# SiLU written with tanh instead of sigmoid, and plain transposes in one part of the attention, in a fused attention and SwiGLU kernel

## The chip, the cores and the metric

The kernel runs on one NeuronCore of a Trainium2 chip. The metric is device time in microseconds (us), the median of several executions. A run also leaves a profile of one execution. Its engines are PE (TensorE matmul), PEld (TensorE weight load), DVE (VectorE), ACT (ScalarE), POOL (GpSimd) and SP (SyncE, which issues transfers here).

## The reference

```python
# q, k, v: 8 batches, 8 heads, 576 rows, 64 columns, float32; tau = 0.02
scores = q @ k.T / 8
thresh = max(scores, axis=-1) - tau
scores = where(scores >= thresh, scores, -1e9)
attn   = exp(scores - max(scores))
attn   = attn / (sum(attn) + 1e-9)
x      = (attn @ v), heads side by side        # 4608 x 512
g      = x @ w_gate                            # 512 x 1536
out    = (g * sigmoid(g) * (x @ w_val)) @ w_out
```

## The kernel before

Attention is worked off in tiles of 128 query rows (the last tile of a batch's head pair has 64 rows of both heads). For each tile TensorE makes scores, VectorE takes the maximum, ScalarE the exponential, VectorE the threshold with its row sum. The feed-forward work of earlier rows is cut into pieces, and a pacing rule puts some of them between the tiles (`fill`), so that TensorE has work while the softmax chain of a tile runs. Score banks (`ps_s`) hold one full tile, so the next tile's scores wait until the threshold instruction has read the last one (19 waits of TensorE, 33.3 us). Four more PSUM banks (`ps_f`) serve everything else.

The first batch has no feed-forward work at first and is computed with whole rows; its probabilities are turned by TensorE. Each turn is a matmul against a diagonal that holds the reciprocals of the row sums, so it normalises at the same time. The turn of a tile's probabilities is called its flip here:

```python
diags = dbufs[0][:, 0:m, :]                       # in scores(), first batch
for x in range(m):
    nc.scalar.activation(diags[:, x, :], ident, AF.Copy, scale=ri[:, x:x + 1])
...
end = ps_f.tile([P, 512], F32, ...)               # in flip()
for h, (p, diag) in enumerate(ps):
    tp = ps_f.tile([P, 512], F32, ...)
    for kt in range(KT):                          # four blocks of 128 x 128
        nc.tensor.matmul(tp[:, kt * P:(kt + 1) * P], p[:, kt * P:(kt + 1) * P], diag, start=True, stop=True)
    nc.tensor.matmul(end[...], p[:, KM:S], diag, ...)
    nc.scalar.copy(pT[:, h], tp...)
```

Later batches ("halved" tiles) use VectorE's transposes (`L371`, 754 ns for 128x576), and GpSimd and ScalarE normalise (`L352`, `L354`) before them.

The gate part copies the gate out of PSUM; the value part multiplies the value by the raw gate; the sigmoid comes later, in groups, because a change between it and the exponential costs a table load; the trace has 38 at `L520` and 37 at `L525`, 1283 ns each:

```python
nc.scalar.copy(gts[...], ps)                                          # gate()
nc.vector.tensor_tensor(out=hts[f // 2], in0=gts[...], in1=ps, op=ALU.mult)   # value()
...
def sigmoids():
    ...                                                    # returns when nothing waits
    eng = nc.vector if attended else nc.gpsimd
    for hts, gt, own in unsig:
        nc.scalar.activation(gt, gt, AF.Sigmoid)           # L520, with a table load before
        for y, (x, ht) in enumerate(own):
            eng.tensor_tensor(out=ht, in0=ht, in1=gt..., op=ALU.mult)         # L522
    if not attended:
        nc.scalar.activation(idle, tau_s, AF.Exp)          # L525, loads the exponential's tables back
    ...                                                    # differences for a seven-product scheme, GpSimd
# main loop, per tile:
    next(go); fill(part); next(go)
    if len(unsig) >= SIG:        # SIG = 3
        sigmoids()
    fill(part); next(go)         # this step emits L352 and L354
```

## Time and profile before

| | before |
|---|---|
| median of 3 runs | 1570.57 us (1569.39 to 1570.74) |
| TensorE busy | 1509.2 of 1568.6 us (96%) |
| ScalarE, VectorE, GpSimd busy | 832, 1022, 628 us |

The groups by line, of which these are the ones that the change touches (columns: line, engine, operation, output and input, count, then busy us and mean ns of one, then idle us of the engine before them and who ended it):

```profile
L504 DVE TENSOR_TENSOR ht<-gt,pv 128x512 f32<-128x512 f32 x102 | 69.8, 685 | 125.0 <-PE pv L481 116.2 <-ACT sums L275 5.9 <-ACT gt L497 2.4
L497 ACT COPY gt<-pg 128x512 f32<-128x512 f32 x108 | 63.5, 588 | 79.7 <-PE pg L481 77.3 <-POOL pall L352 1.8
L520 ACT ACT_TABLE_LOAD x38 | 48.8, 1283 | 8.2 <-DVE ht L504 6.5 <-DVE tot L343 1.1
L525 ACT ACT_TABLE_LOAD x37 | 47.5, 1283 | 0.7
L389 PE MATMUL tp<-pall 128*128 128x128 f32 x288 | 43.5, 296 | 1.3 <-ACT xall L418 0.8 <-ACT pall L361 0.4 <-ACT gt L497 0.2
```

The 75 table loads take 96 us of ScalarE, and the turning matmuls (tp) take 43.5 us of TensorE, the full engine. Whether ScalarE's 96 us matter is a question of waits. The waits of TensorE (who waited for whom, us, times, longest):

```profile
PE sc L296 <- DVE pall L336: 33.3, 19, 3.4
PE sc L301 <- DVE qT L768: 8.0, 1, 8.0
...
PE po L595 <- POOL ht L522: 4.8, 1, 4.8
```

The 8.0 us are the start. Nearly all the rest of TensorE's waiting is for the threshold instruction to free the score banks (3.8 us more of it stand under L301), and once for a gate multiply on GpSimd. No table load is named.

### The profile page before, as it was taken

To read this page: it belongs to the slowest core of one execution; us is meant where nothing else is said; L and a number is where in the kernel's file an instruction comes from. 1 tells how busy PE (TensorE), PEld (TensorE's weight loads), DVE (VectorE), ACT (ScalarE), POOL (GpSimd) and SP (SyncE) were. 2 spreads that over 40 slices of the span, in tenths; PEclk is the share of its full clock that TensorE was granted. 3 is DMA by queue.
4 is the path that set the end of the run, shared out by engine and by line. 5 is a ranking of instruction groups with operands and counts; after the bars stand their busy time and mean duration, and the time that the engine had idled before them with its cause. 6 is when DMAs were issued, how large, how long until landed. Compare 5 with 4: busy or idle time off the path is not lost. (4 is left out here: it accounts for less than half of the span.)

```text
span 1568.6 us, 31607 instructions
## 1 busy us (share of the span) xinstructions
PE 1509.2 (96%) x11872; PEld 1141.3 (73%) x11872; DVE 1022.2 (65%) x3150; ACT 832.2 (53%) x2165; POOL 628.3 (40%) x638
## 2 busy tenths in 40 slices
PE   7999878999999999999999999999999999899998
PEld 5777554467677767777777777777777777788887
DVE  6866877777677757774767777777676777412212
ACT  5767766546465555654555555474647464511110
POOL 2313543336546354633454544363536263500011
PEclk9999999999999999999999999999999999999999
DMA  8533311211111111110211111111011120000000
GB/s 189 142 99 102 95 28 31 56 43 30 24 45 45 31 32 45 43 34 1 45 32 45 31 45 31 45 32 36 12 42 31 45 46 15 1 14 0 14 14 14
DMA packets 176489, 66.93 MB, mean 43 GB/s; under 512 B 159696, under 2 KB 159696, under 8 KB 176336
## 3 DMA queue, kind: packets, MB, share of 16 engines
q1 hardware_dynamic: 168656, 54.88, 15.7%
q0 software_dynamic: 2944, 9.44, 1.7%
q8 instruction: 94, 1.54, 0.4%
q10 hardware_dynamic: 4736, 0.59, 0.3%
q14 instruction: 59, 0.48, 0.1%
HBM read 55.44 MB, written 9.44 MB: 41 GB/s over the span
## 5 line engine op out<-in xcount | busy, mean ns | idle before, releaser
L481 PE MATMUL pv<-xall,wgv 128*128 128x256 f32 x1728 | 405.7, 386 | 0.0
L481 PE MATMUL pg<-xall,wgv 128*128 128x256 f32 x1728 | 399.9, 382 | 0.0
L481 PEld LDWEIGHTS pv<-xall,wgv 128*128 128x128 f32 x1728 | 328.4, 192 | 67.0 <-issue 21.7
L481 PEld LDWEIGHTS pg<-xall,wgv 128*128 128x128 f32 x1728 | 323.5, 190 | 66.4 <-issue 19.0
L352 POOL TENSOR_SCALAR pall<-pall,ri 128x288 f32<-128x288 f32 x252 | 249.9, 1002 | 258.3 <-DVE ri L346 234.0
L336 DVE SCALAR_TENSOR_TENSOR pall<-sc,th,pall 128x288 f32<-128x288 f32 (+1 forms) x540 | 258.6, 529 | 63.6 <-ACT pall L332 63.6
L332 ACT ACTIVATE pall<-sc,nm 128x288 f32<-128x288 f32 (+1 forms) x540 | 236.1, 509 | 0.5
L296 PE MATMUL sc<-kT,qT 64*32 64x288 f32 x4032 | 161.6, 416 | 34.8 <-DVE pall L336 33.3
L316 DVE TENSOR_REDUCE mx<-sc 128x2 f32<-128x576 f32 x252 | 177.7, 742 | 22.3 <-PE sc L296 21.1
L371 DVE STREAM_TRANSPOSE pall<-pall 128x576 f32<-128x576 f32 x252 | 181.9, 754 | 10.7 <-POOL pall L352 10.7
L522 POOL TENSOR_TENSOR ht<-ht,gt 128x512 f32<-128x512 f32 x84 | 104.7, 1272 | 200.9 <-ACT gt L520 200.9
L275 ACT COPY sums<-sums 32x4 f32<-32x4 f32 (+1 forms) x560 | 108.5, 194 | 143.7 <-DVE pall L336 134.2
L595 PE MATMUL po<-wo,ht 128*128 128x256 f32 x768 | 176.8, 382 | 0.0
L595 PEld LDWEIGHTS po<-wo,ht 128*128 128x128 f32 x768 | 144.9, 191 | 28.0 <-issue 4.6
L354 ACT ACTIVATE pall<-pall,ri 128x288 f32<-128x288 f32 x252 | 122.2, 527 | 69.6 <-DVE ri L346 68.5
L504 DVE TENSOR_TENSOR ht<-gt,pv 128x512 f32<-128x512 f32 x102 | 69.8, 685 | 125.0 <-PE pv L481 116.2
L328 ACT ACTIVATE th<-nm,cut 128x4 f32<-128x4 f32 (+1 forms) x140 | 41.2, 295 | 206.1 <-DVE nm L319 206.0
L296 PEld LDWEIGHTS sc<-kT,qT 64*32 64x32 f32 x4032 | 58.6, 106 | 114.7 <-issue 83.5
L438 PE MATMUL xa<-pall,vall 64*64 64x288 f32 x2016 | 130.2, 405 | 0.7 <-issue 0.6
L438 PEld LDWEIGHTS xa<-pall,vall 64*64 64x64 f32 x2016 | 77.8, 133 | 49.1 <-issue 5.8
L608 POOL TENSOR_TENSOR ht<-ht,xall 128x256 f32<-128x256 f32 x48 | 34.7, 726 | 184.5 <-PE po L595 182.2
L497 ACT COPY gt<-pg 128x512 f32<-128x512 f32 x108 | 63.5, 588 | 79.7 <-PE pg L481 77.3
(102 smaller groups left out, 1477.0 us busy)
## 6 DMA issues: line engine op xcount, KB each, us to landing
vall<-in_v_dram SPq DMA_DIRECT2D x112, 144.0 KB, 3.4
qraw<-in_q_dram SPq DMA_DIRECT2D x116, 72.0 KB, 2.5
kraw<-in_k_dram SPq DMA_DIRECT2D x116, 72.0 KB, 2.9
out_dram<-ob POOLq DMA_DIRECT2D x32, 256.0 KB, 2.4
wo<-in_moe_w_gate_dram SPq DMA_DIRECT2D x16, 384.0 KB, 3.8
wo<-in_moe_w_val_dram SPq DMA_DIRECT2D x16, 384.0 KB, 4.3
xall<-in_moe_w_out_dram SPq DMA_DIRECT2D x5, 768.0 KB, 4.6
wo<-in_moe_w_out_dram SPq DMA_DIRECT2D x3, 768.0 KB, 4.8
```

The source lines that it names most:

```text
L275: nc.scalar.copy(out, in_[:, :, 0])
L296: nc.tensor.matmul(ps[g * G:(g + 1) * G, h, 0:SH], qT[hs, col + a * G:col + (a + 1) * G], kT[hs, c * SH:(c + 1) * SH], start=True, stop=True)
L316: nc.vector.tensor_reduce(out=mx[:, 2 * x:2 * x + 2, 0], in_=tile_[:, :, 0:SH], axis=AX.X, op=ALU.max, negate=True)
L332: nc.scalar.activation(ps[x], scs[x], AF.Exp, bias=nm[:, x:x + 1])
L336: nc.vector.scalar_tensor_tensor(out=ps[x], in0=scs[x], scalar=th[:, x:x + 1], in1=ps[x], op0=ALU.is_ge, op1=ALU.mult, accum_out=sm[:, x, ...
L352: nc.gpsimd.tensor_scalar(out=ps[x], in0=ps[x], scalar1=ri[:, x:x + 1], scalar2=None, op0=ALU.mult)
L354: nc.scalar.activation(ps[x], ps[x], AF.Copy, scale=ri[:, x:x + 1])
L371: nc.vector.transpose(out=p, in_=p)
L438: nc.tensor.matmul(xa[a][h * D:(h + 1) * D, at:at + n * G].rearrange("d (i q) -> d i q", q=G), vr[rs, h, j, :], p[rs, lo:lo + n, j, :], st ...
L481: nc.tensor.matmul(ps[:, i], wgv[:, mat, c, (f + i) * P:(f + i + 1) * P], x[:, c, cs], start=(c == 0), stop=(c == NCC - 1))
L522: eng.tensor_tensor(out=ht, in0=ht, in1=gt[:, 2 * y:2 * y + 2, :], op=ALU.mult)
L595: nc.tensor.matmul(ps, h(f), w[:, f, :], start=(f == 0), stop=(f == NF2 - 1))
```

## The change

The intent: g·sigmoid(g) = (g/2)·(tanh(g/2) + 1), and tanh should need no table load beside the exponential's. ScalarE makes tanh(g/2) and g/2 from PSUM, VectorE joins (tanh + 1)·value in one instruction, GpSimd multiplies by g/2. The gates are handed to GpSimd at the end of each tile's slot and not in groups of three. In the second part of the first batch (tiles 2 to 4), ScalarE and GpSimd normalise the probabilities, and TensorE turns them with plain transposes.

```diff
-        nc.scalar.copy(gts[f // per][:, f % per:f % per + GR, :], ps)
+        nc.scalar.activation(gts[f][1], ps, AF.Tanh, scale=0.5)
+        nc.scalar.activation(gts[f][0], ps, AF.Copy, scale=0.5)
...
-        nc.vector.tensor_tensor(out=hts[f // 2][:, :, 0:n], in0=gts[...], in1=ps, op=ALU.mult)
+        nc.vector.scalar_tensor_tensor(out=hts[f // 2], in0=tn, scalar=1.0, in1=ps, op0=ALU.add, op1=ALU.mult)
...
-        for hts, gt, own in unsig:
-            nc.scalar.activation(gt, gt, AF.Sigmoid)
-            for y, (x, ht) in enumerate(own):
-                eng.tensor_tensor(out=ht, in0=ht, in1=gt[:, 2 * y:2 * y + 2, :], op=ALU.mult)
-        if not attended:
-            nc.scalar.activation(idle, tau_s, AF.Exp)
+        for hts, x, gt in ungated:
+            eng.tensor_tensor(out=hts[x], in0=hts[x], in1=gt, op=ALU.mult)
... (main loop)
-            if len(unsig) >= SIG:
-                sigmoids()
             fill(part)
             next(go)
+            gates()
... (scores)
-        if halved:
+        if t >= TA or halved:                      # TA = 2
             for x in range(m):
                 if x % 2:
                     nc.gpsimd.tensor_scalar(out=ps[x], in0=ps[x], scalar1=ri[:, x:x + 1], ...)
                 else:
                     nc.scalar.activation(ps[x], ps[x], AF.Copy, scale=ri[:, x:x + 1])
... (flip)
+                if unit is ident:
+                    nc.tensor.transpose(tp[:, ks], p[:, ks], unit)
+                else:
+                    nc.tensor.matmul(tp[:, ks], p[:, ks], unit, start=True, stop=True)
```

Buffers: five gate buffers become four, and two for tanh are new; the identity matrix moves into a free place of the attention's arena.

More of the change, by code (lines that the diff above doesn't have):

```diff
@@ L82 @@
     hp = ctx.enter_context(tc.tile_pool(name="hp", bufs=8))
-    gp = ctx.enter_context(tc.tile_pool(name="gp", bufs=5))
+    gp = ctx.enter_context(tc.tile_pool(name="gp", bufs=4))
+    tp_ = ctx.enter_context(tc.tile_pool(name="tp", bufs=2))
     op = ctx.enter_context(tc.tile_pool(name="op", bufs=1))
@@ L99 @@
     nc.vector.scalar_tensor_tensor(out=cut, in0=tau_s, scalar=-1.0, in1=cap, op0=ALU.mult, op1=ALU.min)
-    idle = const.tile([P, 1], F32, name="idle")
     sums = deque(const.tile([P, 4, 3], F32, name=f"sums{i}") for i in range(4))
@@ L107 @@
     nc.vector.memset(minus2, -2.0)
-    ident = const.tile([P, P], F32, name="ident")
-    make_identity(nc, ident)
     vall = const.tile([P, 2 * NJ * D], F32, name="vall")
@@ L114 @@
     pall = const.tile([P, 2 * NR - 2, S], F32, name="pall")
+    free = NP * (S - TA * P)
+    ident = pall.rearrange("p n s -> p (n s)")[:, free:free + P]
+    make_identity(nc, ident)
     arenas = [pall[:, 0:NR, :], pall[:, NR - 2:, :]]
@@ L346, in scores @@
         nc.vector.reciprocal(out=ri[:, 0:m], in_=tot[:, 0:m])
-        if not halved:
-            yield
-        if halved:
+        if t >= TA or halved:
             for x in range(m):
@@ L354, in scores @@
                     nc.scalar.activation(ps[x], ps[x], AF.Copy, scale=ri[:, x:x + 1])
+        if not halved:
+            yield
+        if halved:
             unturned.append([seg["p"][:, x, :] for x in at])
         else:
-            diags = dbufs[0][:, 0:m, :]
-            dbufs.rotate(1)
-            for x in range(m):
-                nc.scalar.activation(diags[:, x, :], ident, AF.Copy, scale=ri[:, x:x + 1])
-            unflipped.append((seg, t, [(p.rearrange("p n s -> p (n s)"), diags[:, x, :]) for x, p in enumerate(ps)]))
+            units = [ident] * m
+            if t < TA:
+                units = [dbufs[0][:, x, :] for x in range(m)]
+                dbufs.rotate(1)
+                for x in range(m):
+                    nc.scalar.activation(units[x], ident, AF.Copy, scale=ri[:, x:x + 1])
+            unflipped.append((seg, t, [(p.rearrange("p n s -> p (n s)"), unit) for p, unit in zip(ps, units)]))
             yield
@@ L385, in flip @@
         end = ps_f.tile([P, 512], F32, name="end", tag="psf")
-        for h, (p, diag) in enumerate(ps):
+        for h, (p, unit) in enumerate(ps):
             tp = ps_f.tile([P, 512], F32, name="tp", tag="psf")
             for kt in range(KT):
-                nc.tensor.matmul(tp[:, kt * P:(kt + 1) * P], p[:, kt * P:(kt + 1) * P], diag, start=True, stop=True)
+                ks = slice(kt * P, (kt + 1) * P)
+                if unit is ident:
+                    nc.tensor.transpose(tp[:, ks], p[:, ks], unit)
+                else:
+                    nc.tensor.matmul(tp[:, ks], p[:, ks], unit, start=True, stop=True)
             if t < NT:
-                nc.tensor.matmul(end[h * D:(h + 1) * D, 0:P], p[:, KM:S], diag, start=True, stop=True)
+                nc.tensor.matmul(end[h * D:(h + 1) * D, 0:P], p[:, KM:S], unit, start=True, stop=True)
                 nc.scalar.copy(pT[:, h], tp.rearrange("p (t q) -> p t q", q=P))
@@ L394, in flip @@
                 for hs in (slice(0, D), slice(D, P)):
-                    nc.tensor.matmul(end[hs, 0:D], p[hs, KM:S], diag[hs, hs], start=True, stop=True)
+                    nc.tensor.matmul(end[hs, 0:D], p[hs, KM:S], unit[hs, hs], start=True, stop=True)
                 nc.scalar.copy(pT, tp.rearrange("p (t h q) -> p h t q", h=2, q=D))
@@ L459, in attend @@
         yield
-    unsig = []
+    ungated = []
     attended = []
-    def rows_per(n):
-        return 2 if n > P else 4
     GR = 2
@@ L487, in gate @@
     def gate(j, cs, f, hts, gts):
-        n = cs.stop - cs.start
-        per = rows_per(n)
         if f // 2 not in hts:
             hts[f // 2] = hp.tile([P, 2, TC], F32, name="ht") if j != ("full", 0) else hfirst[:, f:f + 2, :]
-        if f % per == 0:
-            gt = gp.tile([P, 2, TC], F32, name="gt").rearrange("p f n -> p (f n)")
-            gts[f // per] = gt[:, 0:per * n].rearrange("p (f n) -> p f n", n=n)
+        gts[f] = gp.tile([P, GR, TC], F32, name="gt"), tp_.tile([P, GR, TC], F32, name="tn")
@@ L495, in gate @@
         need(NCC * ((f + GR - 1) * P // FW + 1))
         ps = yield from rows_of_products(j, cs, f, 0, "pg")
-        nc.scalar.copy(gts[f // per][:, f % per:f % per + GR, :], ps)
+        nc.scalar.activation(gts[f][1], ps, AF.Tanh, scale=0.5)
+        nc.scalar.activation(gts[f][0], ps, AF.Copy, scale=0.5)
         yield HCOST
     def value(j, cs, f, hts, gts):
-        n = cs.stop - cs.start
-        per = rows_per(n)
         ps = yield from rows_of_products(j, cs, f, 1, "pv")
-        nc.vector.tensor_tensor(out=hts[f // 2][:, :, 0:n], in0=gts[f // per][:, f % per:f % per + GR, :], in1=ps,
-                                op=ALU.mult)
@@ L506, in value @@
-        if f % per == per - GR:
-            unsig.append((hts, gts.pop(f // per), [(x, hts[x][:, :, 0:n]) for x in range((f + GR - per) // 2, f // 2 + 1)]))
+        gt, tn = gts.pop(f)
+        nc.vector.scalar_tensor_tensor(out=hts[f // 2], in0=tn, scalar=1.0, in1=ps, op0=ALU.add, op1=ALU.mult)
+        ungated.append((hts, f // 2, gt))
         if f == NF - GR and cs.stop == TC:
             del xts[j]
-        if f == NF - GR or f == NF - 2 * GR and not ready:
-            sigmoids()
+        if f >= NF - 2 * GR and not ready:
+            gates()
@@ L513, in value, with gates @@
         yield HCOST
-    def sigmoids():
-        if not unsig:
-            return
+    def gates():
         eng = nc.vector if attended else nc.gpsimd
-        for hts, gt, own in unsig:
-            nc.scalar.activation(gt, gt, AF.Sigmoid)
-            for y, (x, ht) in enumerate(own):
-                eng.tensor_tensor(out=ht, in0=ht, in1=gt[:, 2 * y:2 * y + 2, :], op=ALU.mult)
-        if not attended:
-            nc.scalar.activation(idle, tau_s, AF.Exp)
-        for hts, gt, own in unsig:
-            for x, ht in own:
-                if hts["seven"] and x >= NF2 // 2:
-                    x -= NF2 // 2
-                    fs = slice(2 * x, 2 * x + 2)
-                    h11, h21 = hts[x][:, :, 0:P], hts[x][:, :, P:2 * P]
-                    eng.tensor_tensor(out=hs3[:, fs], in0=h11, in1=h21, op=ALU.subtract)
-                    eng.tensor_tensor(out=h21, in0=h21, in1=ht[:, :, P:2 * P], op=ALU.add)
-                    eng.tensor_tensor(out=hs2[:, fs], in0=h21, in1=h11, op=ALU.subtract)
-        unsig.clear()
@@ L538 @@
-    SIG = NF // 4
+        for hts, x, gt in ungated:
+            eng.tensor_tensor(out=hts[x], in0=hts[x], in1=gt, op=ALU.mult)
+        for hts, x, gt in ungated:
+            if hts["seven"] and x >= NF2 // 2:
+                ht = hts[x]
+                x -= NF2 // 2
+                fs = slice(2 * x, 2 * x + 2)
+                h11, h21 = hts[x][:, :, 0:P], hts[x][:, :, P:2 * P]
+                eng.tensor_tensor(out=hs3[:, fs], in0=h11, in1=h21, op=ALU.subtract)
+                eng.tensor_tensor(out=h21, in0=h21, in1=ht[:, :, P:2 * P], op=ALU.add)
+                eng.tensor_tensor(out=hs2[:, fs], in0=h21, in1=h11, op=ALU.subtract)
@@ L539 @@
+        ungated.clear()
     OF = 3
@@ L558, in output @@
                 if f % OF == 0:
-                    if any(u[0] is hts for u in unsig):
-                        sigmoids()
+                    if any(u[0] is hts for u in ungated):
+                        gates()
                     need(NW)
@@ L583, in seven @@
         hts = hidden[unit]
-        if any(u[0] is hts for u in unsig):
-            sigmoids()
+        if any(u[0] is hts for u in ungated):
+            gates()
         ob = op.tile([P, 2, DM], F32, name="ob")
@@ L714 @@
     pbufs = deque(pall[:, 8 + 2 * x:10 + 2 * x] for x in range(2))
-    dbufs = deque(flat[:, NP * (S - QA) + 2 * P * x:NP * (S - QA) + 2 * P * (x + 1)].rearrange("p (h q) -> p h q", h=2)
-                  for x in range(2))
+    dbufs = deque(flat[:, free + (2 * x + 1) * P:free + (2 * x + 3) * P].rearrange("p (h q) -> p h q", h=2) for x in range(2))
     pTbufs = deque(flat[:, (12 + 2 * x) * S:(14 + 2 * x) * S] for x in range(2))
@@ L720 @@
     segs += [{"i": i, "tiles": ([2, 3, 0, 1] if i % 2 else [0, 1, 2, 3]) + [NT], "halved": True} for i in range(NP, NPAIR)]
-    assert (2 * KT + 1) * P <= 2 * S and NP == NT == 4 and NP * (S - QA + P) <= 4 * S
+    assert (2 * KT + 1) * P <= 2 * S and NP == NT == 4 and free + 5 * P <= 4 * S
     gains = []
@@ L825 @@
             next(go)
-            if len(unsig) >= SIG:
-                sigmoids()
             fill(part)
             next(go)
+            gates()
             if attends and n > 2 * NP:
@@ L850 @@
     while fill(HCOST):
-        if unsig:
-            sigmoids()
+        if ungated:
+            gates()
 _INS = ["q", "k", "v", "tau", "moe_w_gate", "moe_w_val", "moe_w_out"]
```

## The prediction

> **What bounds the kernel now.** I read the page first, then stretches of the span, then who waited for whom on TensorE, then the timeline around each of TensorE's long gaps. The page names one full engine:
>
> ```profile
> span 1568.6 us, 31607 instructions
> PE 1509.2 (96%) x11872; PEld 1141.3 (73%) x11872; DVE 1022.2 (65%) x3150; ACT 832.2 (53%) x2165; POOL 628.3 (40%) x638
> ```
>
> TensorE is idle for only 1568.6 - 1509.2 = 59.4 us. So nearly everything that the change takes from ScalarE is taken beside the bound, and the gain has to come from three places: idle time of TensorE that ScalarE or GpSimd causes, TensorE work that disappears, and time at a reduced clock. The view by stretches (columns: length, then busy time and instructions of TensorE, weight load, VectorE, ScalarE, GpSimd, then granted clock, DMA share, GB/s) says where idle time is:
>
> ```profile
> 86.00:165.00 79.00, 77.66 (x634) 58.25 (x632) 52.63 (x113) 57.62 (x121) 24.62 (x15) 1.00 0.36 106
> 160.00:320.00 160.00, 134.80 (x1164) 80.67 (x1160) 128.51 (x414) 101.79 (x275) 67.17 (x58) 0.95 0.23 52
> 320.00:1340.00 1020.00, 1009.34 (x8573) 761.52 (x8558) 725.52 (x2377) 576.63 (x1575) 477.99 (x501) 1.00 0.16 34
> 1340.00:1380.00 40.00, 35.20 (x176) 29.38 (x179) 15.19 (x44) 17.87 (x38) 22.25 (x25) 0.96 0.02 7
> ```
>
> The second part of the first batch (86 to 165 us) is bound by TensorE. From 160 to 320 there is little feed-forward work to fill with, TensorE idles 25 us, and each tile waits for the chain scores, maximum, exponential, threshold, which frees the score banks. The next thousand microseconds hold only 10.7 us of idle, and one gap follows at the end of attention. The waits of TensorE on the page and by pair are almost all one kind, "sc L296 <- DVE pall L336" (33.3 us in 19 waits), plus "po L595 <- POOL ht L522" (4.8 us, once). Two causes show in the timelines. First, table loads before the exponential:
>
> ```profile
> 226.82 0.16 DVE L319 TENSOR_REDUCE nm<-mx 128x4 f32<-128x8 f32 x1
> 227.40 1.28 ACT L525 ACT_TABLE_LOAD   x1
> 228.69 0.20 ACT L525 ACTIVATE idle<-tau_s 128x1 f32<-128x1 f32 x1
> 229.84 1.64 ACT L332 ACTIVATE pall<-sc,nm 128x288 f32<-128x288 f32 x4
> 231.85 0.48 PE L296 MATMUL sc<-kT,qT 64*32 64x288 f32 x8 [3.41 <-DVE pall L336]
> ```
>
> The maximum is ready at 226.98, the exponential starts at 229.84 because ScalarE loads tables and catches up; TensorE stands 3.41 us. Second, GpSimd's gate burst ahead of the normalising multiply:
>
> ```profile
> 398.88 0.73 POOL L535 TENSOR_TENSOR xall<-ht 128x256 f32<-128x256 f32 x1
> 399.59 2.96 POOL L352 TENSOR_SCALAR pall<-pall,ri 128x288 f32<-128x288 f32 x3
> 401.60 0.78 DVE L371 STREAM_TRANSPOSE pall<-pall 128x576 f32<-128x576 f32 x1 [3.20 <-POOL pall L352]
> 403.37 0.72 PE L296 MATMUL sc<-kT,qT 64*32 64x288 f32 x16 [2.86 <-DVE pall L336]
> ```
>
> Three gates of the burst end at 399.6, only then L352 runs, VectorE's in-order queue stands on the transpose, and TensorE waits 2.86 us. The same picture precedes the 2.58 us gap at 568.7.
>
> Idle time also costs twice. Eight stretches of 3.41 us, each soon after such a gap (182, 206, 247, 271, 319, 404, 571, 1363), have a granted clock of 0.50, for instance:
>
> ```profile
> 404.22:407.64 3.41, 3.39 (x21) 2.10 (x22) 2.48 (x10) 1.69 (x7) 2.00 (x3) 0.50 0.02 5
> ```
>
> Each loses about 3.41 x 0.5 = 1.7 us although TensorE counts as busy.
>
> [...]
>
> **The change part by part.**
>
> *ScalarE.* Gone: 75 loads (48.8 + 47.5 = 96.3 us), 37 dummy exponentials (7.5) and 108 sigmoids (62.3). The gate copies stay, with a scale (63.5). Added: 108 tanh from PSUM, at the 588 ns of the copy of the same shape, 63.5 us. In the second part of the first batch, 20 diagonals of 417 ns (8.3) give way to 12 normalising copies of 576 columns at about 0.77 us (L354 takes 527 ns for 288; the 288 more cost some 0.24), 9.2 us. Net about -102 us, 832 to 730. Off the path except in the gaps below.
>
> *VectorE.* The join becomes a scalar_tensor_tensor. From L336, 0.53 us at 288 columns and 0.82 at 576, I take 0.755 at 512 against 0.685: 108 x 0.07 = +7.6 us, beside TensorE.
>
> *GpSimd.* The gate multiply is as before (1272 ns); eight normalising multiplies of 576 columns (about 1.69 us, as the scaling of q) add 13.5 us, in a stretch where GpSimd is busy 24.6 of 79. More important is the order: gates now come after the slot's normalising multiplies and slot by slot, not as a burst of three ahead of them.
>
> *TensorE.* The pace of the fill depends on costs that don't change, so its instruction order stays. Of 36 groups of four transposed blocks (32 copies at L392, 4 at L396), those of tiles 2, 3 and 4 change: 4 pairs x (2 + 2 + 1) = 20 groups, 80 blocks. The 288 matmul instructions are two per block:
>
> ```profile
> 103.65 1.16 PE L389 MATMUL tp<-pall 128*128 128x128 f32 x8
> 104.74 0.43 PE L391 MATMUL end<-pall 128*64 128x128 f32 x2
> ```
>
> Eight take 104.74 - 103.65 = 1.09 us until the next starts; single starts lie 111 ns apart. A transpose as one instruction saves one such step per block: 80 x 0.111 = 8.9 us. [...] That stretch has TensorE busy 77.7 of 79 us and the others at most 57.6, so the saving should reach the end.
>
> **The sum.** Gaps with a table load in the chain: at 178.2 (2.89 us; the maximum is ready 1.5 to 2 us before the exponential) -1.5; at 228.4, -2.6; at 243.5 (2.82; then VectorE's transpose limits) -1.5. Gaps behind the burst: 400.5 and 568.7, -2.9 and -2.6. The gap at 1359 (4.80 us, of which 1.28 is a load and 0.63 a sigmoid, and the join before it waited for GpSimd's L352) should close: -4.8. Together 15.9 us. Clock stretches that go with them: four of eight, 404, 571, 1363 and one of 182 or 247, 4 x 1.7 = 6.8. Transposes 9. That is 31.7. I take off about 4 for new small waits: the tanh holds a gate bank and the ScalarE queue 0.6 us longer, and the latency-bound stretch shifts rather than shrinks wherever the next link is VectorE. Remaining: 28 us, 1570.6 - 28 = 1542 us, 1.8% less.
>
> **Rivals.** (1) *Nothing but the transposes counts*, since ScalarE is 53% busy and TensorE 96%: 9 us, 1561. For it: most gaps in the 160 to 320 stretch (195.4, 202.0, 268.3, 303.7, 316.4; some 11 us) have no table load near. Against it: the exponential visibly standing behind loads at 228 and the gap at 1359. (2) *A new wait replaces the old*: tanh plus copy delay the ScalarE link that VectorE's row sums stand on, or flips wait for GpSimd's 1.69 us multiply where a 0.42 us diagonal was enough. The flips come 1 to 3.5 us after the diagonals (diagonal at 109.59, flip at 112.77), and GpSimd starts right at the reciprocal, in parallel with ScalarE; I expect at most some tenths per tile. If it bites, 1550 to 1556. (3) *Everything closes*: [...]most clock stretches gone, the small gaps after 430 too: 1528 to 1532. VectorE or GpSimd as a new bound I rule out at 66% and 41% busy.
>
> **Range and chances.** The central sum lands just short of 2% (1539.2 us). A spread of some 10 us gives 1529 to 1556 for eight in ten, 0.38 for faster by over 2%, 0.60 for within 2%, 0.02 for slower; only a systematic new wait in all 140 halved tiles would make it slower.
>
> **What would show it.** In the changed profile: one table load left; ScalarE near 730 us, VectorE near 1030; transposes of tiles 2 to 4 as 80 instructions and the stretch up to the first halved tile some 9 us shorter; gaps near 228, 400, 569 and 1359 gone or under 1 us; half-clock stretches down from eight to four or five; TensorE idle near 44 us. The prediction is wrong if transposes take the old 223 ns per block, if score waits on L336 keep their sum with another cause behind them, or if new waits on GpSimd appear at the flips.

## The result, and the profile after

| | before | after |
|---|---|---|
| median (6 runs each) | 1569.97 us (1568.85 to 1570.74) | 1535.26 us (1533.48 to 1539.92) |
| ratio, with 95% interval | | 0.9785 (0.9769 to 0.9800): faster |
| profiled span | 1568.6 us | 1532.6 us |

A ratio is the mean time of one kernel's fast runs over that of the other's of the same rounds, so it is not quite the ratio of the medians. The saving is 34.7 us by medians, where 28 were predicted; the time lies in the range, a little beyond the 2% line that the prediction's centre fell short of. So it is in the class that the prediction had given 0.38, and not in the one given 0.60.

From the page of the changed kernel, the busy times:

```profile
PE 1487.4 (97%) x11792; PEld 1126.1 (73%) x11792; DVE 1024.3 (67%) x3150; ACT 729.7 (48%) x2045; POOL 644.4 (42%) x646
```

TensorE's busy time fell by 21.8 us and its idle time by 14.2 (59.4 to 45.2). ScalarE gave up 102.5 us, as predicted (-102), but this figure alone would tell nothing about the 34.7. The groups by line that answer to those of before:

```profile
L506 DVE SCALAR_TENSOR_TENSOR ht<-tn,pv 128x512 f32<-128x512 f32 x102 | 69.8, 685 | 149.9 <-PE pv L486 147.1 <-ACT sums L277 2.6
L500 ACT ACTIVATE gt<-pg 128x512 f32<-128x512 f32 x108 | 65.0, 602 | 0.0
L499 ACT ACTIVATE tn<-pg 128x512 f32<-128x512 f32 x108 | 64.9, 601 | 152.7 <-PE pg L486 152.0
...
L396 PE MATMUL tp<-pall 128*128 128x128 f32 x80 | 13.1, 286 | 3.6 <-ACT xall L427 3.6
L333 ACT ACT_TABLE_LOAD x1 | 1.3, 1283 | 7.8 <-DMA extra<-in_k_dram 7.8
```

One load is left. The join of three operands costs exactly what the join of two did, 685 ns. 80 transposes stand where 160 matmul instructions stood, and an idle time of 3.6 us has appeared in front of them. The same in TensorE's waits:

```profile
PE sc L298 <- DVE pall L338: 20.7, 14, 2.9
...
PE tp L396 <- ACT xall L427: 3.6, 2, 1.8
PE pg L486 <- ACT xall L427: 1.3, 1, 1.3
```

Score waits fell from 33.3 to 20.7 us, the wait for the gate multiply is gone, and 4.9 us of waits for an evacuation on ScalarE (L427) are new.

**Where the 36 us are.** Apart from the turning matmuls, TensorE executes the same 11584 matmul instructions in the same order in both traces. So the start of the same instruction can be subtracted, trace from trace. I call this the lead of the changed kernel. By stage:

| stage, in time of before (us) | lead gained (us) | predicted (us) |
|---|---|---|
| 0 to 70, start and first part of the first batch | 1.4 | 0 |
| 70 to 165, tiles with transposes | 6.1 | 9 |
| 165 to 322, little feed-forward work | 6.9 | 5.6 and a clock stretch of 1.7 |
| 322 to 398 | 0.1 | 0 |
| 398 to 408, gap at 400.5 and its half clock | 4.9 | 4.6 |
| 408 to 565 | 0.3 | 0 |
| 565 to 575, gap at 568.7 and its half clock | 4.3 | 4.3 |
| 575 to 1340 | 5.0 | 0 |
| 1340 to 1367, end of attention | 6.5 | 6.5 |
| deducted for new waits | | -4 |

Half clock means a stretch of 3.41 us whose granted clock is 0.50 in the trace; it costs an estimated 1.7 us (3.41 x 0.5).

The stages sum to 35.6 before rounding, and 0.4 come at the very end. The stretches of the changed kernel's trace that answer to the prediction's (the second and third start where the same TensorE instructions start):

```profile
82.60:157.50 74.90, 69.82 (x570) 49.40 (x568) 54.45 (x112) 52.90 (x108) 34.49 (x21) 1.00 0.38 114
153.00:305.70 152.70, 132.66 (x1153) 79.50 (x1156) 128.15 (x414) 90.27 (x260) 65.77 (x57) 0.96 0.25 56
305.70:1310.95 1005.25, 1002.92 (x8573) 760.27 (x8558) 725.12 (x2377) 500.15 (x1493) 482.30 (x504) 1.00 0.16 34
```

In the first, TensorE is now idle for 5 of 75 us, where before it was idle for 1.3 of 79. In the third 2.3 us of idle are left of 10.7. At the gap that had been 3.41 us long, near 228 us, the timeline of the changed kernel shows the chain without a load in it:

```profile
218.65 0.16 DVE L321 TENSOR_REDUCE nm<-mx 128x4 f32<-128x8 f32 x1
...
219.05 1.66 ACT L334 ACTIVATE pall<-sc,nm 128x288 f32<-128x288 f32 x4
...
221.15 0.72 PE L298 MATMUL sc<-kT,qT 64*32 64x288 f32 x16 [0.93 <-DVE pall L338]
```

From the maximum's end to the exponential's start it is now 0.24 us (219.05 - 218.81), where it was 2.86; the gap is 0.93 us.

### The profile page after: what moved, and what is told of

Same layout as the page of the kernel before. It is cut to its first block, busy times and chain, and to the rows that moved or that the text cites. A ratio compares the mean times of both kernels' runs of the same rounds, so it can differ in the third digit from the quotient of the medians.

```text
span 1532.6 us, 31424 instructions
## 1 busy us (share of the span) xinstructions
PE 1487.4 (97%) x11792; PEld 1126.1 (73%) x11792; DVE 1024.3 (67%) x3150; ACT 729.7 (48%) x2045; POOL 644.4 (42%) x646
## 4 chain that ended last, share of the span: by engine, by line
PE 85%; DVE 9%; ACT 2%; issue 1%; DMA 1%; SPq 1%; POOLq 0%; POOL 0%; DVEq 0%; ACTq 0%
PE pv L486 24%; PE pg L486 23%; PE po L587 19%; PE xa L447 8%; PE sc L298 8%; DVE pall L338 2%; DVE mx L318 2%; DVE pall L376 1%; DVE mx L274 1%; ACT pall L334 1%; DMA vall<-in_v_dram 1%; PE tp L396 1%; ACT sums L277 1%; SPq L242 0%; PE xa L421 0%
## 5 line engine op out<-in xcount | busy, mean ns | idle before, releaser
L352 POOL TENSOR_SCALAR pall<-pall,ri 128x288 f32<-128x288 f32 (+1 forms) x260 | 265.2, 1030 | 427.3 <-DVE ri L348 376.0
L486 PE MATMUL pv<-xall,wgv 128*128 128x256 f32 x1728 | 401.6, 383 | 0.0
L354 ACT ACTIVATE pall<-pall,ri 128x288 f32<-128x288 f32 (+1 forms) x264 | 132.0, 540 | 104.8 <-DVE ri L348 103.5
L298 PE MATMUL sc<-kT,qT 64*32 64x288 f32 x4032 | 158.6, 413 | 21.7 <-DVE pall L338 20.7
L506 DVE SCALAR_TENSOR_TENSOR ht<-tn,pv 128x512 f32<-128x512 f32 x102 | 69.8, 685 | 149.9 <-PE pv L486 147.1
L499 ACT ACTIVATE tn<-pg 128x512 f32<-128x512 f32 x108 | 64.9, 601 | 152.7 <-PE pg L486 152.0
L518 POOL TENSOR_TENSOR ht<-ht,gt 128x512 f32<-128x512 f32 x84 | 106.6, 1271 | 33.3 <-ACT sums L277 21.4
```

Source lines behind the costliest of these rows:

```text
L298: nc.tensor.matmul(ps[g * G:(g + 1) * G, h, 0:SH], qT[hs, col + a * G:col + (a + 1) * G], kT[hs, c * SH:(c + 1) * SH], start=True, stop=True)
L352: nc.gpsimd.tensor_scalar(out=ps[x], in0=ps[x], scalar1=ri[:, x:x + 1], scalar2=None, op0=ALU.mult)
L354: nc.scalar.activation(ps[x], ps[x], AF.Copy, scale=ri[:, x:x + 1])
L486: nc.tensor.matmul(ps[:, i], wgv[:, mat, c, (f + i) * P:(f + i + 1) * P], x[:, c, cs], start=(c == 0), stop=(c == NCC - 1))
L518: eng.tensor_tensor(out=hts[x], in0=hts[x], in1=gt, op=ALU.mult)
```

## The experiments

All outputs are right. "Before" is the kernel before, run on the same chip in the same rounds; its median lies between 1569.1 and 1570.5 us. The four kernels from tanh_only to old_order shared one chip, the next four another, and the last three a third. A difference between kernels of two groups is read from medians of different rounds, so the ratios should be compared too.

| kernel | median us | ratio to before (95%) |
|---|---|---|
| changed kernel | 1535.3 | 0.9785 (0.9769 to 0.9800) |
| tanh_only | 1540.6 | 0.9819 (0.9802 to 0.9835) |
| transpose_only | 1570.0 | 1.0004 (0.9989 to 1.0019) |
| loads_back | 1544.3 | 0.9840 (0.9826 to 0.9855) |
| old_order | 1537.5 | 0.9799 (0.9785 to 0.9814) |
| late_gate | 1546.0 | 0.9839 (0.9824 to 0.9853) |
| late_gate_loads | 1572.5 | 1.0013 (1.0006 to 1.0020) |
| xa_first | 1532.0 | 0.9750 (0.9734 to 0.9766) |
| transpose_xa_first | 1566.9 | 0.9980 (0.9971 to 0.9988) |
| after_again (changed kernel) | 1534.2 | 0.9779 (0.9764 to 0.9795) |
| xa_first_again | 1530.1 | 0.9754 (0.9740 to 0.9768) |
| all_transposed | 1536.9 | 0.9790 (0.9776 to 0.9803) |

### The two halves apart

tanh_only is the changed kernel with the diagonals back for all tiles of the first batch:

```diff
-        if t >= TA or halved:
+        if halved:
...
-            if t < TA:
+            if t <= NT:
                 units = [dbufs[0][:, x, :] for x in range(m)]
```

> The changed kernel with scaled diagonals and plain matmuls for all tiles of the first batch, as before the change; SiLU by tanh stays. Theory (the lead of one trace over the other, step by step): each of the 20 groups of four blocks gets its 0.50 us back (10.1 us), and three new waits of 1.3 to 1.8 us at the flips vanish (about 3 us), so some 6 to 7 us over the changed kernel: 1541 to 1542 us. Rival (the waits of the score matmuls shift when the first batch is longer, and eat or add to it): 1536 or 1547.

Measured: 1540.6 us, as the theory had it. The transposes are worth 5.3 us on top of the tanh half.

transpose_only is the kernel before, with the normalising and transposing parts of the diff and with its sigmoid untouched:

> The kernel before with the plain transposes and nothing else. Theory: 10.1 us of TensorE gone, 3 to 4 given back in waits at the flips, so 6 to 7 us under the kernel before: about 1563 us, and together with the tanh half it makes up the whole 35 us. Rival (the halves need each other, because sigmoid loads on ScalarE stand in the flips' way): 1567 us or more.

Measured: 1570.0 us, nothing gained; the theory's 1563 is refuted and the rival is right. The lead of this trace over the one of before shows all 20 steps of 0.50 us, 10.1 us, and then less than 1 us of lead after 171 us. In between are four waits for a PSUM bank, at a flip or just after it, of which this one is the kind that the changed kernel does not have (timeline of transpose_only):

```profile
124.20 1.28 ACT L531 ACT_TABLE_LOAD   x1
...
125.60 0.57 ACT L503 COPY gt<-pg 128x512 f32<-128x512 f32 x1
...
126.31 0.63 PE L393 MATMUL tp<-ident,pall 128*128 128x128 f32 x4 [1.44 <-ACT gt L503]
```

The second transpose group of a tile needs a PSUM bank. The bank is freed by a ScalarE copy, and that copy stands behind a table load (here at 125.60, behind the load at 124.20, and TensorE waits 1.44 us). Soon after the waits, two stretches at half clock follow (127.4 and 144.5 us, granted clock 0.50) that the trace of before does not have; they cost an estimated 1.7 us each (3.41 x 0.5). So the halves are not additive: 28.6 us alone, 0 alone, 34.7 together.

### What the loads cost by themselves, and what the order of the gates did

loads_back is the changed kernel with idle switches after every third gate:

```diff
+            done[0] += 1                 # per gate, in gates()
+        if done[0] >= 3 and not attended:
+            done[0] = 0
+            nc.scalar.activation(idle, tau_s, AF.Sigmoid)
+            nc.scalar.activation(idle, tau_s, AF.Exp)
```

> The changed kernel with a dummy sigmoid and a dummy exponential of one element after every third gate, until attention ends: some 70 table loads are back, arithmetic and order are not touched. Theory (loads cost only where ScalarE's delay of an exponential reaches TensorE, in the stretch from 160 to 320 us; the other gaps came from GpSimd's order): gaps of 1.5 to 2.5 us return at three or so places, with at most two half-clock stretches: 6 to 9 us more, 1541 to 1544 us. Rival (the loads were the cause of everything that the transposes did not bring, some 28 us): about 1560 us.

Measured: 1544.3 us, 9.0 more, at the edge of the theory and far from the rival's 1560. Its trace has 58 loads (29 pairs) beside the first one, 74.4 us of ScalarE. The time comes back near 115 us, where the wait for a PSUM bank grew from 1.3 to 2.4 us, in the stretch of little feed-forward work (about 4 us), and later in small pieces. Another 1.2 us lie before 70 us and 1.7 us in a half-clock stretch at 141 us; two executions of one kernel differ by as much (see after_again below), so some 6 us is the surer size. So most of ScalarE's idle switches are hidden: 9.0 us show of 74.4.

old_order is the changed kernel, no load, with the gates where the sigmoids had been:

```diff
             next(go)
+            if len(ungated) >= 3:
+                gates()
             fill(part)
             next(go)
-            gates()
...
-        if f >= NF - 2 * GR and not ready:
+        if f == NF - GR or f == NF - 2 * GR and not ready:
             gates()
```

> The changed kernel with the gates emitted as before the change: in bursts of three, ahead of the slot's second fill and so ahead of its normalising multiplies on GpSimd; no table load comes back. Theory: the waits near 400 and 568 us and at the end of attention return, 2.9, 2.6 and up to 5 us with their half-clock stretches of 1.7 us: 10 to 16 us more, 1545 to 1551 us. Rival (the burst was harmful only because each sigmoid came late behind its load): within 2 us of the changed kernel.

Measured: 1537.5 us, some 2 us more, with intervals that overlap, so that a price of the order is not clear of noise. The theory, which was also the prediction's reading of the gap at 400 us, falls. GpSimd's burst of three multiplies and nine differences does stand ahead of L352 again, but it is over early enough: near 400 there is no wait, near 550 us one of 0.36, and at the end of attention one of 0.6:

```profile
PE sc L298 <- DVE pall L338: 21.1, 15, 2.9
...
PE po L587 <- POOL ht L518: 0.6, 1, 0.6
```

In the kernel before, all three multiplies wait for the load and the sigmoids (the group L522 waited 200.9 us for L520 in 32 waits). In old_order two of them run before the third is joined. GpSimd's burst near 400 us, before and then in old_order (timelines), where the third join ends at 386.92 and at 373.92 us:

```profile
388.99 3.73 POOL L522 TENSOR_TENSOR ht<-ht,gt 128x512 f32<-128x512 f32 x3 [5.87 <-ACT gt L520]
...
369.89 2.51 POOL L518 TENSOR_TENSOR ht<-ht,gt 128x512 f32<-128x512 f32 x2
374.06 1.28 POOL L518 TENSOR_TENSOR ht<-ht,gt 128x512 f32<-128x512 f32 x1 [1.67 <-ACT sums L277]
```

From the third join's end to the start of L352 it is 12.7 us before (to 399.59) and 8.3 us in old_order (to 382.24).

### The gate behind ScalarE, without and with loads

If the order is harmless, then the dependence is left to be tested: the sigmoid was a ScalarE pass between the join and the multiply. late_gate is old_order with such a pass, an in-place copy of the join's result; late_gate_loads adds a load ahead of the group's passes and one behind:

```diff
+        if ungated and not attended:                                   # late_gate_loads only
+            nc.scalar.activation(idle, tau_s, AF.Sigmoid)
         for hts, x, gt in ungated:
+            nc.scalar.activation(hts[x], hts[x], AF.Copy)              # both
             eng.tensor_tensor(out=hts[x], in0=hts[x], in1=gt, op=ALU.mult)
+        if ungated and not attended:                                   # late_gate_loads only
+            nc.scalar.activation(idle, tau_s, AF.Exp)
```

> The kernel with the old order of the gates, and each join's result passes ScalarE once more (an in-place copy of 512 columns) before its multiply on GpSimd, so that the multiply waits for ScalarE as it did for the sigmoid; no table load. Theory A (what closed the gaps near 400 and 568 us and at the end of attention is that the multiply no longer waits for a ScalarE pass behind the join): most of the 10 to 14 us of those gaps comes back, 1547 us or more. Theory B (the pass is harmless without the loads ahead of it): at most 4 us over the old order's 1537.5, so under 1542.

Measured: 1546.0 us, 8.5 over old_order, between the two theories' bounds. Waits return at 389 us (1.75), 556 us (1.62) and at the end of attention (1.74 in place of 0.55). Near 389 us all three multiplies wait for the pass again, and L352 starts 11.4 us after the third join.

The 8.5 us are between chips; by the ratios it is some 6 us. The two traces agree with that: of 8.5 us, 6.4 lie at these three places (with a half-clock stretch after the first), and 1.7 are a half-clock stretch at 96 us, after a flip wait that both kernels have, so it is chance. The pass also gives ScalarE 58 us more work, which could delay the exponentials; but from 165 to 322 us, where they are on the chain, the two traces part by only 0.1 us.

> The same with a table load before the passes and one after, as the sigmoid had them. This rebuilds the schedule of the kernel before with tanh arithmetic and plain transposes, so it should come near the transposes-only kernel: 1565 to 1571 us. Theory A leaves about half of the distance from 1537 to 1570 to the loads, theory B nearly all of it. If it stays under 1555, something else in the tanh half saves time.

Measured: 1572.5 us, 26.5 more, 1.5 us over the expected range. The loads are three quarters of the distance from 1537.5 us, between theories A and B. This rebuilds about the time of transpose_only (1570.0), and also the list of its TensorE waits:

```profile
PE sc L299 <- DVE pall L339: 35.4, 20, 3.5
...
PE po L593 <- POOL ht L522: 3.7, 1, 3.7
```

So the ladder from the changed kernel back is: order of the gates 2.3 us (not clear of noise), a ScalarE pass between join and multiply 8.5 (6 without chance), table loads in this chain 26.5. The same sort of load costs 9.0 us when only the exponential stands behind it (loads_back) and 26.5 when the gate does too. loads_back has 29 pairs and late_gate_loads 37, which cannot make a threefold difference; but the two also place their loads at slightly different points of the slot, and loads_back keeps the new order of the gates, so the split is a size and not an exact figure. The lead of late_gate over late_gate_loads rises by 1.1 us near each of 974, 1104 and 1133 us: these are the small gaps of before after 430 us, which the prediction had not given to the loads.

### The waits that the transposes brought

These waits look like this in the changed kernel (timeline):

```profile
90.24 0.66 PE L396 MATMUL tp<-pall 128*128 128x128 f32 x4
...
92.08 0.73 ACT L334 ACTIVATE pall<-sc,nm 128x576 f32<-128x576 f32 x1
...
92.70 0.20 ACT L427 COPY xall<-xa 128x64 f32<-128x64 f32 x1
...
93.05 0.63 PE L396 MATMUL tp<-pall 128*128 128x128 f32 x4 [1.78 <-ACT xall L427]
```

At this tile one bank of the four holds a half finished value product, the others the attention result (xa), `end` and the first head's transposes. The second head needs xa's bank. Its copy had been ready to run since xa ended at 90.31, but ScalarE's queue has both exponentials ahead of it. Before the change TensorE came later to this point and waited 0.38 us. xa_first emits that copy ahead of the exponentials:

```diff
         else:                                     # scores(), whole rows, after the maxima
             ...
+        if not halved:
+            yield
         if halved: ...
... (main loop)
             attend_tile()
+            if not seg["halved"]:
+                next(go)                          # now the exponentials
             flip()
```

> The changed kernel; in the first batch the copy that empties the attention result's PSUM bank is emitted ahead of the exponentials on ScalarE instead of behind them. Theory (the waits of 1.8, 1.3 and 1.8 us at the flips are the fourth PSUM bank, held until that copy): all three vanish, 4 to 5 us less, 1530 to 1531.5 us. Rival (the flips wait for the normalised tile or for the exponentials themselves): no gain, 1535 us or more, since the exponentials start up to 0.25 us later.

Measured: 1532.0 us at first (3.2 less) and 1530.1 against 1534.2 us in the direct comparison below. The three waits are gone from the trace; the lead rises by 1.83, 1.41 and 1.83 us there. The timeline at the same tile:

```profile
93.09 0.21 ACT L429 COPY xall<-xa 128x64 f32<-128x64 f32 x1 [0.19 <-PE xa L427]
...
93.92 0.66 PE L398 MATMUL tp<-pall 128*128 128x128 f32 x4
```

No idle time stands behind the second group now. That the bank was the cause is shown.

transpose_xa_first puts the same edit on transpose_only:

> The transposes-only kernel, which gained nothing, with the same earlier copy. Theory (10.1 us of TensorE saved, some 5 us of it lost in waits for the bank and 3.4 us in two half-clock stretches that these waits set off): the waits and the two stretches go, 1570.0 becomes 1561 to 1563 us. Rival (the saving was lost further on, in the latency-bound stretch after 165 us): 1568 us or more.

Measured: 1566.9 us, 3.1 less, between theory and rival. Three of the four waits go, but the one at the sigmoids' loads grows from 1.44 to 3.27 us (for the gate copy L505 on ScalarE), and a half-clock stretch follows at 125.9 us. With sigmoid loads on ScalarE, one bank still comes free too late for the faster flips, though the copy of xa no longer stands in the way.

### The changed kernel again, and more transposes

> The changed kernel unaltered, on the same chip as the next two, so that they can be compared with it: 1533 to 1540 us as before, a wider spread than the kernel before has, since where the half-clock stretches fall differs from run to run.

Measured: 1534.2 us (1533.5 to 1539.5). The slowest of these was the profiled one (mean granted clock 0.994, the other three 0.996 to 0.997), and its trace shows what its extra 5 us are. It has the same waits at the flips as the first trace, but after those at 92.9 and 139.6 us a half-clock stretch follows, for instance:

```profile
142.20:145.60 3.40, 3.40 (x10) 2.70 (x9) 3.27 (x6) 2.94 (x5) 2.51 (x2) 0.50 0.04 16
```

The first trace has none there. What the traces show is where the waits fall. The half-clock stretches of one trace start at whole multiples of 3.413 us from one another (before: 182.36, 206.25, 247.21 and 271.10 us, so 7, 19 and 26 from the first; changed kernel: 181.32, 198.39, 256.41 and 304.20 us, so 5, 22 and 36); I call these steps, counted on through the trace, its grid. In the step before each of these two stretches (91.03 to 94.44 and 138.81 to 142.23) TensorE was busy for 1.82 and 1.63 us. In the first trace the same waits straddle a line of its grid, and the windows that hold most of them (89.16 to 92.57 and 136.95 to 140.36) have 2.10 and 2.08 us busy. How much idle time it takes to set off a stretch is not shown by these four windows. Two such stretches make an estimated 3.4 us (2 x 3.41 x 0.5), and 1.6 us differ at the start (before 34 us) between the two executions of one kernel. So the 1.4 us of lead that the table gives to the start are within what the same kernel shows from run to run, and not credited to the change.

> The changed kernel with the earlier copy, again: 3 us under the unaltered one (its trace lacks 5.1 us of waits at the flips and has one half-clock stretch more). If it is less than 1.5 us, the first comparison was spread.

Measured: 1530.1 us, 4.1 less than the unaltered kernel on the same chip: the better version holds.

all_transposed makes the condition true for every tile of the first batch, on top of xa_first:

```diff
-        if t >= TA or halved:
+        if True:
...
-            if t < TA:
+            if False:
```

> The earlier copy, and plain transposes for all tiles of the first batch, tiles 0 and 1 too: 16 more groups at 0.50 us, 8 us of TensorE. Theory (from about 20 us on that part is bound by TensorE, 39 of 40 us busy): 5 to 8 us less than the earlier copy alone, 1524 to 1527 us. Rival (in that part the normalising pass on GpSimd, 1.7 us, stands behind the scaling of q and the joining of weights, and the flips wait for it): no gain, or up to 5 us more.

Measured: 1536.9 us, 6.7 more than xa_first; the theory is refuted. Each group saves its 0.50 us, but flips now wait for GpSimd (timeline of all_transposed):

```profile
25.31 4.08 POOL L354 TENSOR_SCALAR pall<-pall,ri 128x576 f32<-128x576 f32 x2
...
27.43 0.69 PE L398 MATMUL tp<-pall 128*128 128x128 f32 x4 [4.38 <-POOL pall L354]
```

The normalising pass of the second head came behind the scaling of q, which had waited 7.60 us for its transfer. Half-clock stretches follow at 27.9 us and, twice as long, at 48.4 us (mean granted clock of the four runs 0.991 to 0.993, of xa_first_again's five 0.995 to 0.997). The restriction to tiles 2 to 4 is right.

## Why the prediction was right, and where it was not

- **The place of the gain** was right: TensorE's order stayed, ScalarE's 102 us were off the path, and the gain came from gaps, clock and transposes. The range was 28 us with some 13 either way; 34.7 came, inside it. The class did not come as thought: 0.60 stood on a result within 2%, and the gain is 2.15%. Most of what came beyond the centre is the missed term below. The ScalarE sum (730 predicted, 729.7 measured) was exact, the VectorE term was not: 0 in place of +7.6 us for the join (685 ns in both traces). It lay beside TensorE and cost nothing. Two small slips change nothing: 1570.6 - 28 is 1542.6 and not 1542, and the scaling of q takes 1.73 us in the trace where 1.69 was read.
- **Gaps with a load in the chain** at 228.4 and 243.5: -2.6 and -1.5 predicted, leads of 2.5 and 1.6 measured. At 178.2 the lead rose by 1.6 too, but with half-clock stretches falling elsewhere nearby it went up and down by about 2 us until 198.
- **Gaps at 400 and 568 and at the end of attention**: sizes right (4.9, 4.3 and 6.5 us with their half-clock stretches), cause partly wrong. The step that failed is "GpSimd's gate burst ahead of the normalising multiply" as a cause of its own, cured by the order. Without a ScalarE pass in the chain the order is worth some 2 us at most. What made the burst late was the gate multiply standing behind ScalarE's load and sigmoids; the dependence and the loads in it make up the rest.
- **Transposes**: "the saving should reach the end" failed. One instruction a block, the author's estimate, held (80 for 80 blocks). The gross term was slightly low (0.50 us a group, from 1.09 us to the next instruction before to 0.59 after; 10.1 us in place of 8.9), but 4.2 us were given back in the same stretch by waits for a PSUM bank. Net 5.3 us in the runs, and nothing at all without the tanh half. The prediction's rival (2) had the form right, a wait at the flips, but looked for it at GpSimd's multiply; it was the copy behind the exponentials.
- **The deduction of 4 us for new waits** is about the 4.2 found, though not in the places named, so that agreement is luck. The half-clock stretches did fall from eight (182.36 to 1363.37 us) to four (181.32 to 304.20 us) within the work, all at a granted clock of 0.50, as predicted.
- **Missed term**: 5.0 us between 575 and 1340 us. Small gaps near 972, 1102 and 1131 us, and many steps below 0.4 us, came from the loads as well (between late_gate and late_gate_loads this stage changes by 6.9 us); I had left them out because no load stood close enough to the gap.
- **Open**: whether the new order alone would have closed the gaps while the sigmoid and its loads still stood before the multiply, which no run tried; how the 26.5 us of the loads divide between the exponential's and the gate's delay beyond the size that loads_back gives; and the 6.9 us of 165 to 322, which sum many gains and losses as the half-clock stretches move.

## What to carry to other kernels

TensorE was 96% busy here, and of the 102.5 us that ScalarE gave up only what stood behind TensorE's waits and its reduced clock reached the time (28.6 us for the tanh half). A wait's named releaser is only the last link: follow the queue behind it to the instruction that made it late. Time taken from the full engine itself was not safe either: the transposes saved 10.1 us of TensorE, and the time fell by 5.3 us with the tanh half and by nothing without it, because TensorE arrived earlier at the next shared buffer. Look at which queue frees that buffer, and put the freeing copy ahead of long work in that queue (3.2 and 4.1 us less here). To name a cause, rebuild the old schedule from the new kernel one step at a time; the order alone, the dependence alone and the loads in the dependence had three quite different prices here (2.3, 8.5 and 26.5 us).
